# The first layer's function as a clamped square: one ScalarE pass and two VectorE passes from PSUM, in a new order

## The chip, the cores and the metric

The kernel runs on one core of one Trainium2 chip. The metric is the device time of one execution in microseconds (us), as the median of several runs. Engines are TensorE (PE; PEld are its weight loads), VectorE (DVE), ScalarE (ACT), GpSimd (POOL) and SyncE (SP), which issues the DMAs here.

## What is computed

An attention with a memory term over 4 batches of 8 heads, 576 positions and 64 channels, followed by two feed-forward layers of 512 to 2048 to 512 channels over the 2304 rows. The first one has the function that this change is about:

```
h = x @ w_in
g = where(h >= 1, h, where(h <= -1, 0, (h + 1)**2 / 4))
x = g @ w_out
```

The second layer is `(max(h, 0) + alpha * min(h, 0)) @ w_out`. All is float32 outside; inside, the matrices are held as a high and a low float16 half, and each product is made of three float16 products (high by high, high by low, low by high).

## The kernel before

The work is written once in Python as named sections: `p` prepares a batch, `a` attends, `w` converts weights, `s` makes the scales, `u` is the first layer's first product with its function, `d` its second product, `t` and `f` the second layer. A planner (`Plan`) collects the instructions and puts them in order before anything is issued: `schedule` is a list scheduler that walks over time with a cost for each instruction, and `RANK` is a written list of 534 section parts that gives the priorities, and so the order in which each engine gets its instructions. Where an instruction may run on several engines (`plan.either`), the table `HOME` fixes the engine for some of them, and the planner picks for the rest. Instructions inside `with plan.ahead()` stand before all others in the ranking. On the chip each engine works through its own list in order.

A batch has two chunks of 288 columns. `up1` makes, for each of eight `fq`, a PSUM tile `h` of 128 x 2 x 288 (two banks) out of 24 products of `w1i` with `x`. PSUM tiles with the tag `f` have two buffers; `h`, the outputs `y` of `down1` and the tiles of the second layer share them. The function needs the tile `h` and scales that are given by channel: `su`, `sd` (128 x 8, one column for each `fq`), `bu` and `c` (one column). It is worked out like this, with everything scaled by a power of two so that float16 holds it:

```
A.activation(out=u, in_=ps[:, :, :n], func=AF.Relu, scale=su[:, fq : fq + 1], bias=bu[:, 0:1])
A.activation(out=d, in_=ps[:, :, :n], func=AF.Prelu, scale=sd[:, fq : fq + 1], bias=bu[:, 1:2], alpha=0.5)
shift(d, c)
V.scalar_tensor_tensor(out=u, in0=u, scalar=c, in1=d, op0=ALU.min, op1=ALU.mult)
split(u, gh, gl)
```

Two ScalarE passes read PSUM, `shift` adds `c` to `d` on ScalarE, VectorE or GpSimd, and VectorE multiplies. `split` copies `u` to float16 (`gh`, on any of the three) and subtracts it (`gl`, on GpSimd or VectorE). `u` and `d` are in SBUF, 128 x 576 float32, with two buffers each. `down1` then multiplies `g` with `w1o`, 4 x 48 products a chunk. `scales1` works out the small scale tiles once a batch. `attend` makes scores `s`, their exponentials `e`, probabilities `p` (transposed by DMA into `pt`, or on TensorE into `tt` for the first batch) and the attention products `px`. The four first-layer batches and the weights for the second layer are interleaved with the attention of the later batches; the second layer comes last.

Every line of the profile is line 424 (where the planned instructions are issued), so tiles tell the instructions apart.

Of the kernel before, what the change touches and what calls it, by code (L numbers as in the profile page):

```python
# [1222 lines left out]
a1C2.2 u01.1 a1C2.4 a1C2.1 a1C3.1 d00.o3 w1i3.3 a1C3.0 s3 a1C1.1 a1C1.0 a1C3.2 a1C1.2 a2C0.1 p1.3 d10 w1o0.3 a1C3.4
a0B1 a1C3.3 w1o1.s0 w1o2.1 d00.o2 u01.4 u01.0 p2.s u01.6 d01.o1 w1i1.s0 u01.5 w1i1.s1 d01.o0 a2C1.2 a2C1.1 u10.4
a2C1.0 w1o1.2 a2C0.2 a2C1.3 a2C1.4 a2C0.4 a2C0.3 d01.o3 a2C3.3 a2C3.0 d01.o2 a2C0.0 u10.6 a2C3.4 u10.1 u10.0 a2C2.1
a2C3.2 u10.2 a2C3.1 u10.3 a2C2.0 w1o1.0 p2.0 u10.5 u11.1 u10.7 d10.o0 a2C2.4 d10.o1 a2C2.2 a2C2.3 w1o3.2 a3C0.0 a3C1.3
u11.6 m3.0 d10.o2 u11.3 a3C0.1 p3.s w1o0.0 a3C1.4 w1i3.s1 d10.o3 d21 u11.5 w1o3.s0 u11.7 a3C0.2 w2i0.0 m3.2 u11.0
a3C0.x4 a3C1.0 u11.2 u11.4 d11.o0 d11.o1 m1.2 w2i0.a a0B2.x4 a3C0.4 a3C0.3 w1i1.0 d11.o3 u20.3 a3C3.4 a3C1.1 u20.4
w1i0.2 m3.1 a3C1.2 a1C2.q w1i3.s0 p2 a3C2.2 a1C2 a3C1 w1i2.3 u21.2 a3C2.1 w2i0.1 a3C3.q d11.o2 a2C0.q u20.7 a0B2
a3C2.x2 m1.1 u20.0 w2i0.s1 a2C0.x2 a3C2.4 m2.1 a3C3.3 u21.3 w2i2.s1 a0A2.x2 a3C2.0 u20.5 w1i2.s0 d11 u20.1 a3C3.1  # L1230
w2i0.m a3C1.x2 u20.2 u21.7 a3C2.x4 a2C0.x4 u20.6 a3C0.q a3C3.0 a2C2.q w2i2.0 a2C1.q u21.4 d20.o0 d20.o3 p2.3 w1i0.3
w1o3.s1 d20.o1 u21.5 d20.o2 a3C3.2 a1C1 a1C0.x2 u21.1 w2i2.a a3C2.3 w2i1.s0 w2i3.3 u21.0 u21.6 w2i2.m d21.o0 w2i1.s1
w2i1.a d21.o1 u30.1 d21.o2 a1C1.x4 d21.o3 u30.0 u30.6 u31.2 w2i2.2 m3.3 w2i3.a w1o1.1 w2i2.s0 w2i1.2 w2i3.s0 w1i3.a
f01 u30.4 w2i3.m c u30.2 u30.7 a2C3.x2 u30.3 m2.2 u31.1 w1o1.3 w2o3.a w1o2.3 w2i2.1 p2.1 w2i1.m u30.5 w2o0.1 u31.5
d30.o2 d30.o0 w2o3.m f00 w1o0.s0 w2o0.a d30.o1 d30.o3 w2o3.3 a1C3 w2o3.2 u31.0 a2C0 w2i1.3 w2o0.m w2i3.2 w2o1.m u31.7
w1o2.2 p2.2 a3C1.q u31.3 u31.4 f00.2 f00.3 u31.6 f00.7 a2C1 d31.o1 f00.6 w2o2.2 s1 d31.o0 w2o0.s0 d31.o3 w2o3.s0
d31.o2 w2o3.s1 w1i2.a f00.1 a2C3 w1o1.s1 a2C2 w1o3.3 f00.4 f00.0 a0A0 f01.7 f00.5 f01.5 f01.6 p3.1 d01 d30 f00.o1
# [152 lines left out]
```

## Time and profile before

| | |
|---|---|
| median of 3 runs | 1044.4 us (1041.12 to 1047.64) |
| profiled execution | 1042.5 us, span of its instructions 1040.6 us |
| TensorE busy | 947.1 us, 91% of the span |
| VectorE, ScalarE, GpSimd busy | 684.7, 515.6, 375.7 us |
| mean granted TensorE clock | 0.993 of full speed |

The busy time of an engine is the time in which one of its instructions ran. TensorE does nearly the same products whatever the function; the time in which it is idle is what the rest of the kernel adds. Times in windows are counted from the start of the span.

### The profile page before, as it was taken

To read this page: it belongs to the slowest core of one execution; us is meant where nothing else is said; L and a number is where in the kernel's file an instruction comes from. 1 tells how busy PE (TensorE), PEld (TensorE's weight loads), DVE (VectorE), ACT (ScalarE), POOL (GpSimd) and SP (SyncE) were. 2 spreads that over 40 slices of the span, in tenths; PEclk is the share of its full clock that TensorE was granted. 3 is DMA by queue.
4 is the path that set the end of the run, shared out by engine and by line. 5 is a ranking of instruction groups with operands and counts; after the bars stand their busy time and mean duration, and the time that the engine had idled before them with its cause. 6 is when DMAs were issued, how large, how long until landed. Compare 5 with 4: busy or idle time off the path is not lost.

```text
span 1040.6 us, 20570 instructions
## 1 busy us (share of the span) xinstructions
PE 947.1 (91%) x8043; PEld 709.2 (68%) x8043; DVE 684.7 (66%) x1803; ACT 515.6 (50%) x1030; POOL 375.7 (36%) x405
## 2 busy tenths in 40 slices
PE   2178779999999999999989999999999999999998
PEld 1156446666667666766667777777777777777776
DVE  6979989989887788987877889892323413042320
ACT  5458777667566663765456646332322423131220
POOL 1353554667466673543533521251010111100020
PEclk9999988999999999999999999999999999999999
DMA  9833324567755774376654152320001000000000
GB/s 334 291 113 122 135 89 135 129 133 184 164 126 112 162 164 94 71 157 124 118 145 146 48 171 82 129 86 24 30 18 35 12 13 12 24 1 23 7 18 23
DMA packets 132096, 104.23 MB, mean 100 GB/s; under 512 B 98464, under 2 KB 113312, under 8 KB 132000
## 3 DMA queue, kind: packets, MB, share of 16 engines
q1 hardware_dynamic: 132000, 102.93, 36.9%
q8 instruction: 63, 1.03, 0.4%
q14 instruction: 33, 0.27, 0.1%
HBM read 66.73 MB, written 9.44 MB: 73 GB/s over the span
## 4 chain that ended last, share of the span: by engine, by line
PE 40%; DVE 4%; DMA 3%; POOL 2%; issue 2%; ACT 1%; SPq 0%; ACTq 0%; POOLq 0%
PE h L424 21%; PE o L424 17%; PE y L424 3%; DMA pt<-p 1%; DMA w2o_raw<-in_w2o 1%; DVE u L424 1%; DMA w2i_raw<-in_w2i 1%; POOL d L424 1%; POOL w2o L424 0%; DVE p L424 0%; ACT u L424 0%; DVE yt L424 0%; DMA yr<-y 0%; POOL p L424 0%; ACT d L424 0%
## 5 line engine op out<-in xcount | busy, mean ns | idle before, releaser
L424 PE MATMUL y<-g,w1o 128*128 128x288 f16 x1536 | 203.7, 286 | 1.8 <-DVE g L424 1.5
L424 PE MATMUL h<-x,w1i 128*128 128x288 f16 x1536 | 200.5, 286 | 4.6 <-ACT d L424 2.1
L424 PE MATMUL h<-yt,w2i 128*128 128x288 f16 x1536 | 194.8, 286 | 1.3 <-ACT u L424 1.3
L424 PE MATMUL o<-g,w2o 128*128 128x288 f16 x1536 | 193.9, 286 | 0.5 <-POOL w2o L424 0.5
L424 DVE SCALAR_TENSOR_TENSOR u<-u,al 128x288 f32<-128x288 f32 x128 | 67.0, 555 | 186.8 <-ACT u L424 186.6
L424 PEld LDWEIGHTS <-w1i 128*128 128x128 f16 x1536 | 146.9, 98 | 50.9 <-issue 12.7
L424 PEld LDWEIGHTS <-w1o 128*128 128x128 f16 x1536 | 145.0, 98 | 51.3 <-issue 12.6
L424 PEld LDWEIGHTS <-w2i 128*128 128x128 f16 x1536 | 150.1, 98 | 39.3 <-issue 1.5
L424 PEld LDWEIGHTS <-w2o 128*128 128x128 f16 x1536 | 150.1, 98 | 38.6 <-POOL w2o L424 0.8
L424 POOL TENSOR_TENSOR g<-u,g 128x576 f16<-128x576 f32 x54 | 74.1, 1372 | 182.7 <-ACT g L424 132.6
L424 ACT ACTIVATE e<-e,mxt 128x576 f32<-128x576 f32 (+4 forms) x160 | 88.3, 553 | 65.6 <-DVE mxt L424 55.1
L424 ACT ACTIVATE u<-h,sa 128x288 f32<-128x288 f32 x128 | 58.5, 498 | 125.5 <-PE h L424 122.3
L424 POOL TENSOR_SCALAR g<-u 128x576 f16<-128x576 f32 x40 | 30.5, 764 | 213.4 <-DVE u L424 156.9
L424 PE MATMUL s<-qk 64*128 64x288 f32 (+4 forms) x384 | 89.7, 481 | 15.8 <-DVE mxt L424 14.2
L424 DVE TENSOR_TENSOR g<-u,g 128x576 f16<-128x576 f32 x74 | 59.9, 810 | 31.5 <-ACT g L424 18.7
L424 ACT ACTIVATE oe<-o,osc 128x288 f32<-128x288 f32 x32 | 16.0, 501 | 111.4 <-PE o L424 111.4
L424 DVE SCALAR_TENSOR_TENSOR u<-u,c,d 128x576 f32<-128x576 f32 x64 | 59.7, 934 | 14.4 <-POOL d L424 10.1
L424 DVE CUSTOM_DVE_ANT_0 e<-s,mask 128x288 f32<-128x288 f32 (+4 forms) x160 | 64.3, 419 | 6.6 <-PE s L424 4.2
L424 PEld LDWEIGHTS s<-qk 64*128 64x128 f32 x384 | 40.0, 203 | 42.0 <-DVE mxt L424 27.4
L424 ACT ACTIVATE u<-h,bu,su 128x576 f32<-128x576 f32 x64 | 52.8, 825 | 21.8 <-PE h L424 16.6
L424 ACT ACTIVATE g<-u 128x576 f16<-128x576 f32 x61 | 41.6, 681 | 43.8 <-DVE u L424 23.2
L424 DVE SCALAR_TENSOR_TENSOR p<-e,sm,p 128x320 f16<-128x320 f32 (+4 forms) x80 | 57.0, 730 | 8.2 <-POOL p L424 5.8
(221 smaller groups left out, 1247.4 us busy)
## 6 DMA issues: line engine op xcount, KB each, us to landing
ring<-in_w1i SPq DMA_DIRECT2D x16, 512.0 KB, 6.2
w1o_raw<-in_w1o SPq DMA_DIRECT2D x16, 512.0 KB, 3.7
w2i_raw<-in_w2i SPq DMA_DIRECT2D x16, 512.0 KB, 3.8
w2o_raw<-in_w2o SPq DMA_DIRECT2D x16, 512.0 KB, 3.8
qk<-in_qk SPq DMA_DIRECT2D x12, 576.0 KB, 4.6
qn<-in_qn SPq DMA_DIRECT2D x16, 320.0 KB, 3.4
vc<-in_vc SPq DMA_DIRECT2D x16, 320.0 KB, 4.3
y<-ye SPq DMA_DIRECT2D x32, 144.0 KB, 2.5
```

What stands on the lines that cost most here:

```text
L424: fn(*args, **kw)
```

## The change

The function is worked out as the larger of two values: the product times a scale, and the square of the product after it was clamped to the two limits (where h is -1 and 1). VectorE clamps the tile out of PSUM into `d`, with two limits by channel (`lim`, new in `scales1`); ScalarE squares `d` in place, with scale and bias by channel; VectorE reads PSUM a second time, scales it and takes the larger of it and `d`. `shift` goes. `bu` has one column instead of two, `sd` has the scale `c` twice, and `sc[b]` holds `lim` where `c` was. `RANK` and `HOME` are replaced as a whole. Among the parts `uNN.N` and `dNN.oN` and `fNN` of `RANK`, a first-layer tile follows another directly in 46 places before and in 43 after. Of the instructions of `u` parts that `HOME` fixes, copies to float16 were 18 on ScalarE, 11 on VectorE and 22 on GpSimd and are 17, 14 and 17; subtractions were 29 on VectorE and 16 on GpSimd and are 22 and 23.

```diff
@@ -512,15 +512,6 @@
                 V.tensor_copy(out, src)
             else:
                 V.tensor_scalar(out=out, in0=src, scalar1=scale, scalar2=None, op0=ALU.mult)
-
-        plan.either(*(lambda e=e: way(e) for e in engines))
-
-    def shift(t, by, engines=(A, V, G)):
-        def way(e):
-            if e is A:
-                A.activation(out=t, in_=t, func=AF.Identity, bias=by)
-            else:
-                e.tensor_scalar(out=t, in0=t, scalar1=by, scalar2=None, op0=ALU.add)
 
         plan.either(*(lambda e=e: way(e) for e in engines))
 
@@ -993,22 +984,32 @@
         V.tensor_scalar(
             out=ig.bitcast(I32), in0=f, scalar1=float(-2 * ONE23), scalar2=float(381 * ONE23), op0=ALU.mult, op1=ALU.add
         )
-        bu = tiny.tile([P, 2], F32, tag="bu", name=f"bu_{b}")
-        V.tensor_scalar(out=bu[:, 0:1], in0=c, scalar1=0.5, scalar2=None, op0=ALU.mult)
-        V.tensor_scalar(out=bu[:, 1:2], in0=c, scalar1=-1.0, scalar2=None, op0=ALU.mult)
+        bu = tiny.tile([P, 1], F32, tag="bu", name=f"bu_{b}")
+        V.tensor_scalar(out=bu, in0=c, scalar1=0.5, scalar2=None, op0=ALU.mult)
+
+        lim = tiny.tile([P, 2, 8], F32, tag="lim", name=f"lim_{b}")
+        V.tensor_scalar(
+            out=lim[:, 1].bitcast(I32),
+            in0=inv1.bitcast(I32),
+            scalar1=-1.0,
+            scalar2=float(254 * ONE23),
+            op0=ALU.mult,
+            op1=ALU.add,
+        )
+        V.tensor_scalar(out=lim[:, 0], in0=lim[:, 1], scalar1=-1.0, scalar2=None, op0=ALU.mult)
         su = tiny.tile([P, 8], F32, tag="su", name=f"su_{b}")
         sd = tiny.tile([P, 8], F32, tag="sd", name=f"sd_{b}")
-        V.tensor_scalar(out=su, in0=inv1, scalar1=bu[:, 0:1], scalar2=None, op0=ALU.mult)
-        V.tensor_scalar(out=sd, in0=inv1, scalar1=c, scalar2=None, op0=ALU.mult)
+        V.tensor_scalar(out=su, in0=inv1, scalar1=bu, scalar2=None, op0=ALU.mult)
+        V.tensor_scalar(out=sd, in0=inv1, scalar1=c, scalar2=c, op0=ALU.mult, op1=ALU.mult)
         ym = tiny.tile([P, NCH * EB], F32, tag="ym", name=f"ym_{b}")
-        sc[b] = (c, ig, bu, su, sd, ym)
+        sc[b] = (lim, ig, bu, su, sd, ym)
 
     def split(u, gh, gl):
         copy(gh, u, None, (A, V, G))
         combine(gl, u, gh, ALU.subtract)
 
     def up1(b, ch, w_in, tags=("g", "g", "g", "g")):
-        c, ig, bu, su, sd, ym = sc[b]
+        lim, ig, bu, su, sd, ym = sc[b]
         x = x_t[b][ch]
         n = CHS[ch][1]
         g = []
@@ -1023,19 +1024,25 @@
             u = buf([P, 2, n], F32, "u", f"u{b}_{ch}_{fq}")
             d = buf([P, 2, n], F32, "d", f"d{b}_{ch}_{fq}")
             with plan.ahead():
-                A.activation(out=u, in_=ps[:, :, :n], func=AF.Relu, scale=su[:, fq : fq + 1], bias=bu[:, 0:1])
-
-
-                A.activation(
-                    out=d, in_=ps[:, :, :n], func=AF.Prelu, scale=sd[:, fq : fq + 1], bias=bu[:, 1:2], alpha=0.5
+
+
+                V.tensor_scalar(
+                    out=d,
+                    in0=ps[:, :, :n],
+                    scalar1=lim[:, 0, fq : fq + 1],
+                    scalar2=lim[:, 1, fq : fq + 1],
+                    op0=ALU.max,
+                    op1=ALU.min,
                 )
-                shift(d, c)
-                V.scalar_tensor_tensor(out=u, in0=u, scalar=c, in1=d, op0=ALU.min, op1=ALU.mult)
+                A.activation(out=d, in_=d, func=AF.Square, scale=su[:, fq : fq + 1], bias=bu)
+                V.scalar_tensor_tensor(
+                    out=u, in0=ps[:, :, :n], scalar=sd[:, fq : fq + 1], in1=d, op0=ALU.mult, op1=ALU.max
+                )
                 split(u, gh, gl)
         return g
 
     def down1(b, ch, g, w_out, w_out_inv):
-        c, ig, bu, su, sd, ym = sc[b]
+        lim, ig, bu, su, sd, ym = sc[b]
         ysc = tiny.tile([P, 4], F32, tag="ysc", name=f"ysc_{b}_{ch}")
         V.tensor_scalar(out=ysc, in0=w_out_inv, scalar1=ig, scalar2=None, op0=ALU.mult)
         n = CHS[ch][1]
@@ -1215,119 +1222,112 @@
 ORDER = _order()
 
 RANK = """
-w1i0.m w1i1.3 u00.0 m1.0 w1i0.s0 s0 a0A1.q d00 p0.1 w1i0.s1 a0A0.x2 w1i0.1 a0A1.0 a0A1.1 a0A0.1 p0.3 a0A0.q a0A3.q
-w1i0.a a0A0.0 p0.s w1i1.m a0A1.2 a0A0.2 a0A2.1 a0A2.0 w1i0.0 l w1i2.m a0A2.2 m1.3 p0 a0A3.0 w1o0.a w1i1.1 a0A3.1
...
+m1.3 w1i0.m p0.3 a0A0.0 l a0A0.x2 s0 a0A1.2 a0A0.1 p0.s d00 a0A1.0 w1i1.m a0A1.1 w1i0.s0 a0A0.2 a0A2.1 a0A3.0 w1i1.3
+a0A2.2 w1i0.s1 a0A3.1 w1i2.m a0A2.0 u00.0 w1i1.1 w1i0.a a0A3.2 a0A0.q p0.0 p1 p0.1 a0B0.3 u00.6 u00.1 a0B0 d10 m1.0
...
```

## Rows read from the trace of the kernel before

**Rows 1.** windows: length; busy us of PE, PEld, DVE, ACT, POOL; clock; DMA share, GB/s
```profile
0.00:94.60 94.60, 44.09 (x225) 28.77 (x225) 74.36 (x254) 54.78 (x125) 33.07 (x45) 1.00 0.67 232
94.60:182.00 87.40, 70.52 (x514) 48.24 (x514) 81.02 (x217) 67.27 (x114) 41.70 (x33) 0.92 0.33 112
182.00:640.00 458.00, 437.29 (x4090) 317.57 (x4089) 382.23 (x1061) 281.46 (x581) 241.59 (x277) 1.00 0.56 130
640.00:1040.60 400.60, 395.25 (x3219) 314.57 (x3216) 147.08 (x272) 112.08 (x212) 59.35 (x52) 1.00 0.10 32
```

**Rows 2.** TensorE's waits, 94.6 to 182 us: total, times, longest
```profile
PE s L424 <- DVE mxt L424: 5.7, 4, 1.8
PE px L424 <- ACT tt L424: 2.5, 2, 1.8
PE w1o_pm L424 <- DVE w1o_mg L424: 2.3, 1, 2.3
```

**Rows 3.** TensorE's waits, 182 to 640 us
```profile
PE px L424 <- DMA pt<-p: 6.9, 9, 1.4
PE s L424 <- DVE mxt L424: 3.9, 6, 1.1
PE px L424 <- DVE x L424: 2.6, 3, 1.4
```

**Rows 4.** TensorE's waits, 0 to 94.6 us
```profile
PE pt L424 <- POOL pf L424: 15.7, 1, 15.7
```

**Rows 5.** groups of instructions by form: count, busy us, mean ns, idle before
```profile
L424 ACT ACTIVATE u<-h,bu,su 128x576 f32<-128x576 f32 x64 | 52.8, 825 | 21.8 <-PE h L424 16.6 <-DVE g L424 1.9 <-DVE w2o_mg L424 1.4
L424 ACT ACTIVATE d<-h,bu,sd 128x576 f32<-128x576 f32 x64 | 52.7, 824 | 4.6 <-PE h L424 4.5
L424 ACT ACTIVATE d<-d,c 128x576 f32<-128x576 f32 x33 | 25.5, 772 | 0.4
L424 POOL TENSOR_SCALAR d<-d,c 128x576 f32<-128x576 f32 x16 | 29.4, 1835 | 13.4 <-ACT d L424 11.9 <-issue 1.4
L424 DVE TENSOR_SCALAR d<-d,c 128x576 f32<-128x576 f32 x15 | 9.3, 620 | 1.9 <-ACT d L424 1.6
L424 DVE SCALAR_TENSOR_TENSOR u<-u,c,d 128x576 f32<-128x576 f32 x64 | 59.7, 934 | 14.4 <-POOL d L424 10.1 <-ACT d L424 2.8 <-ACT u L424 0.8
```

**Rows 6.** groups by form on VectorE, passes that read PSUM
```profile
L424 DVE TENSOR_SCALAR x<-px,xs 128x288 f16<-128x288 f32 x5 | 2.5, 505 | 0.0
L424 DVE SCALAR_TENSOR_TENSOR x<-px,xs,x 128x288 f16<-128x288 f32 x16 | 8.1, 509 | 3.3 <-ACT x L424 3.2
L424 DVE CUSTOM_DVE_ANT_0 e<-s,mask 128x448 f32<-128x448 f32 x32 | 19.3, 613 | 1.0 <-PE s L424 0.9
L424 DVE CUSTOM_DVE_ANT_0 e<-s,mask 128x288 f32<-128x288 f32 x32 | 13.9, 445 | 1.6 <-POOL p L424 1.1 <-PE s L424 0.4
```

**Rows 7.** groups by form on ScalarE
```profile
L424 ACT ACTIVATE oe<-o,osc 128x288 f32<-128x288 f32 x32 | 16.0, 501 | 111.4 <-PE o L424 111.4
L424 ACT ACTIVATE w1i<-w1i_t,w1i_s 128x1024 f16<-128x1024 f32 x4 | 4.6, 1138 | 0.4 <-DVE w1i_t L424 0.4
```

**Rows 8.** instructions of tile d: duration ns min/median/max
```profile
L424 DVE SCALAR_TENSOR_TENSOR u<-u,c,d x64: 797/818/1839, 100.6 to 641.3; 128x576 f32<-128x576 f32 x64
```

**Rows 9.** windows, instructions of tile d: length; busy us of DVE, ACT, POOL
```profile
94.60:182.00 87.40, 7.91 (x9) 9.65 (x12) 6.40 (x3) 0.92 0.33 112
182.00:640.00 458.00, 60.15 (x69) 67.32 (x84) 22.97 (x13) 1.00 0.56 130
```

**Rows 10.** ScalarE's timeline near 583 us: start, us
```profile
583.04 0.83 ACT L424 ACTIVATE d<-h,bu,sd 128x576 f32<-128x576 f32 x1 [0.58 <-PE h L424]
583.78 0.82 ACT L424 ACTIVATE u<-h,bu,su 128x576 f32<-128x576 f32 x1
```

**Rows 11.** chain that ended last, near 583 us: start, us
```profile
583.12 2.94 PE h L424 x24
```

**Rows 12.** groups by form on ScalarE, table loads
```profile
L424 ACT ACT_TABLE_LOAD x1 | 1.3, 1283 | 0.7 <-PEq L1379 0.7
```

More of the change, by code (lines that the diff above doesn't have):

```diff
@@ L1223 @@
[L1223 to L1237, printed above, removed]
@@ L1328 @@
[L1328 to L1330 removed]
+w1i0.0:1=dve w1i0.1:1=act w1i0.s0:1=pool w1i0.s0:2=pool w1i0.3:1=act a0A0.0:1=act a0A0.0:3=dve a0A0.1:2=act
+a0A0.1:3=pool a0A0.1:4=act a0A0.2:1=dve a0A0.2:2=act a0A0.2:3=dve a0A0.2:4=dve a0A0.x2:1=dve a0A0.x2:3=act
@@ new lines @@
+w1i1.1:1=act w1i1.s0:2=dve w1i1.2:1=act w1i1.s1:1=pool a0A1.0:2=act a0A1.1:1=dve a0A1.1:3=pool a0A1.1:4=act
+a0A1.2:1=pool a0A1.2:3=pool a0A1.2:4=act a0A1.x2:1=dve w1i2.0:1=dve w1i2.s0:2=dve w1i2.2:1=dve w1i2.3:1=dve
+w1i2.s1:1=dve w1i2.s1:2=dve a0A2.0:1=act a0A2.0:4=dve a0A2.1:2=pool a0A2.2:2=pool a0A2.2:4=act a0A2.x2:3=dve
+w1i3.1:1=act w1i3.s0:1=pool w1i3.s0:2=dve w1i3.2:1=dve w1i3.3:1=act w1i3.s1:1=act a0A3.0:2=act a0A3.0:3=dve
+a0A3.0:4=act a0A3.1:1=dve a0A3.1:3=dve a0A3.1:4=act a0A3.2:3=dve a0A3.x2:1=act a0A3.x2:3=act u00.0:2=pool u00.1:1=pool
@@ new lines @@
+u00.2:1=act u00.3:1=pool u00.4:1=pool u00.5:1=dve u00.6:1=act u00.7:1=act u00.7:2=pool w1o0.0:1=dve w1o0.s0:1=act
+w1o0.2:1=act w1o0.3:1=act w1o0.s1:1=act w1o0.s1:2=dve w1o1.0:1=act w1o1.s0:2=dve w1o1.2:1=act w1o1.3:1=dve
+w1o1.s1:1=pool w1o1.s1:2=dve w1o2.1:1=act w1o2.2:1=act w1o2.3:1=act w1o3.0:1=dve w1o3.1:1=dve w1o3.s0:2=dve
+w1o3.2:1=act w1o3.s1:2=dve a0B0.3:3=pool a0B0.4:1=act a0B0.4:3=pool a0B0.4:5=dve a0B0.x4:1=act a0B1.3:2=dve
+a0B1.3:3=pool a0B1.4:1=dve a0B1.4:2=act a0B1.4:3=dve a0B1.4:5=act a0B2.3:1=pool a0B2.3:3=dve a0B2.3:4=act a0B2.4:2=act
@@ new lines @@
+a0B2.4:3=pool a0B2.4:4=dve a0B3.3:2=pool a0B3.3:3=pool a0B3.4:2=dve a0B3.4:3=pool a0B3.4:4=act a0B3.4:5=act
+a0B3.x4:1=act u01.0:1=act u01.0:2=dve u01.1:1=act u01.1:2=pool u01.2:1=act u01.2:2=dve u01.3:1=act u01.4:1=act
+u01.4:2=pool u01.5:2=dve u01.6:1=dve u01.7:1=pool a1C0:1=pool a1C0.0:1=pool a1C0.0:3=act a1C0.0:4=dve a1C0.0:5=pool
+a1C0.0:6=dve a1C0.1:1=act a1C0.1:3=act a1C0.1:6=pool a1C0.2:1=dve a1C0.2:3=act a1C0.2:5=pool a1C0.2:6=dve
+a1C0.x2:3=act a1C0.3:2=pool a1C0.3:3=dve a1C0.3:4=dve a1C0.4:1=dve a1C0.4:2=pool a1C0.4:3=act a1C0.4:4=dve
@@ new lines @@
+a1C0.4:6=dve a1C0.x4:1=act a1C1:1=dve a1C1.0:1=act a1C1.0:4=dve a1C1.0:5=pool a1C1.0:6=dve a1C1.1:1=dve a1C1.1:2=pool
+a1C1.1:4=pool a1C1.2:1=pool a1C1.2:3=pool a1C1.2:5=act a1C1.2:6=pool a1C1.x2:1=dve a1C1.3:1=dve a1C1.3:2=pool
+a1C1.3:3=pool a1C1.3:4=dve a1C1.3:5=pool a1C1.4:1=act a1C1.4:2=dve a1C1.4:4=dve a1C1.4:5=pool a1C1.x4:1=dve
+a1C2.0:3=dve a1C2.0:4=pool a1C2.0:5=pool a1C2.1:1=dve a1C2.1:2=pool a1C2.1:5=pool a1C2.2:1=act a1C2.2:2=dve
+a1C2.2:3=pool a1C2.2:5=pool a1C2.2:6=pool a1C2.x2:1=act a1C2.3:1=act a1C2.3:2=dve a1C2.3:3=pool a1C2.3:5=act
@@ new lines @@
+a2C2.1:6=dve a2C2.2:2=dve a2C2.2:3=pool a2C2.2:4=dve a2C2.2:5=dve a2C2.2:6=pool a2C2.x2:1=act a2C2.x2:3=dve
+a2C2.3:1=dve a2C2.3:2=dve a2C2.3:4=dve a2C2.3:5=act a2C2.4:2=dve a2C2.4:3=pool a2C2.4:6=pool a2C2.x4:1=act a2C3:1=dve
+a2C3.0:1=pool a2C3.0:2=pool a2C3.0:3=act a2C3.0:4=pool a2C3.0:6=dve a2C3.1:1=dve a2C3.1:4=pool a2C3.1:6=pool
+a2C3.2:1=dve a2C3.2:2=pool a2C3.2:3=act a2C3.2:5=pool a2C3.x2:1=act a2C3.x2:3=dve a2C3.3:1=pool a2C3.3:4=dve
+a2C3.3:5=dve a2C3.3:6=pool a2C3.4:1=pool a2C3.4:2=pool a2C3.4:3=act a2C3.4:4=dve a2C3.4:6=dve a2C3.x4:1=act
@@ new lines @@
+u10.0:1=dve u10.0:2=dve u10.1:1=pool u10.2:1=act u10.3:1=dve u10.3:2=dve u10.4:1=act u10.4:2=pool u10.5:1=pool
+u10.5:2=pool u10.6:2=dve u10.7:2=dve u11.0:2=dve u11.1:2=dve u11.2:1=dve u11.2:2=pool u11.3:1=dve u11.3:2=pool
+u11.4:2=dve u11.5:2=pool u11.6:2=pool u11.7:1=pool a3C0.0:1=pool a3C0.0:2=dve a3C0.0:4=dve a3C0.0:5=act a3C0.0:6=pool
+a3C0.1:1=dve a3C0.1:2=dve a3C0.1:5=pool a3C0.1:6=pool a3C0.2:1=act a3C0.2:3=pool a3C0.2:6=pool a3C0.3:1=act
+a3C0.3:2=dve a3C0.3:3=pool a3C0.3:5=pool a3C0.3:6=pool a3C0.4:1=dve a3C0.4:3=pool a3C0.4:4=dve a3C0.4:5=dve
@@ new lines @@
+a3C0.x4:1=act a3C1:1=dve a3C1:2=dve a3C1.0:1=pool a3C1.0:2=pool a3C1.0:3=dve a3C1.0:4=dve a3C1.0:5=pool a3C1.1:1=dve
+a3C1.1:2=dve a3C1.1:3=pool a3C1.1:4=dve a3C1.1:5=dve a3C1.1:6=pool a3C1.2:3=act a3C1.x2:1=act a3C1.x2:3=act
+a3C1.3:2=pool a3C1.3:3=act a3C1.3:4=dve a3C1.3:6=pool a3C1.4:1=act a3C1.4:2=dve a3C1.4:3=act a3C1.4:4=dve a3C1.4:5=dve
+a3C1.4:6=dve a3C2:1=act a3C2:2=dve a3C2.0:1=pool a3C2.0:3=act a3C2.0:4=pool a3C2.0:5=pool a3C2.1:3=act a3C2.1:4=dve
+a3C2.1:6=pool a3C2.2:1=dve a3C2.2:3=dve a3C2.2:4=pool a3C2.2:6=dve a3C2.x2:3=act a3C2.3:1=dve a3C2.3:3=dve
@@ new lines @@
+a3C2.3:4=pool a3C2.3:5=pool a3C2.3:6=pool a3C2.4:1=dve a3C2.4:2=pool a3C2.4:4=dve a3C2.4:5=pool a3C2.4:6=dve
+a3C2.x4:1=act a3C3:1=pool a3C3:2=dve a3C3.0:2=dve a3C3.0:3=pool a3C3.0:5=dve a3C3.0:6=pool a3C3.1:2=pool a3C3.1:3=dve
+a3C3.1:4=pool a3C3.1:5=act a3C3.2:1=pool a3C3.2:2=dve a3C3.2:4=dve a3C3.2:5=act a3C3.x2:1=act a3C3.x2:3=act
+a3C3.3:1=dve a3C3.3:4=dve a3C3.3:5=act a3C3.4:2=dve a3C3.4:4=pool a3C3.4:5=pool a3C3.4:6=pool a3C3.x4:1=act
+u20.0:1=dve u20.0:2=pool u20.1:1=dve u20.1:2=pool u20.2:1=pool u20.2:2=pool u20.3:1=act u20.4:1=act u20.4:2=pool
@@ new lines @@
+u20.5:1=pool u20.5:2=dve u20.6:1=pool u20.6:2=dve u20.7:1=act u20.7:2=dve u21.0:2=dve u21.1:1=dve u21.2:1=dve
+u21.3:1=pool u21.3:2=pool u21.4:1=dve u21.4:2=dve u21.5:1=dve u21.5:2=pool u21.6:1=act u21.6:2=dve u21.7:2=dve
+w2i0.0:1=act w2i0.1:1=dve w2i0.s0:1=act w2i0.2:1=act w2i0.3:1=dve w2i0.s1:2=dve w2i1.0:1=act w2i1.s0:1=act
+w2i1.s1:1=act w2i2.0:1=act w2i2.1:1=dve w2i2.s0:1=act w2i2.2:1=dve w2i2.3:1=act w2i3.1:1=dve w2i3.s0:1=pool
+w2i3.2:1=dve w2i3.3:1=dve w2i3.s1:1=act w2i3.s1:2=pool u30.0:1=pool u30.0:2=dve u30.2:1=pool u30.2:2=dve u30.3:1=pool
@@ new lines @@
+f01.2:1=act f01.2:2=pool f01.4:1=pool f01.5:1=pool f01.6:2=dve f01.7:1=pool f01.7:2=dve f10.0:1=pool f10.0:2=dve
+f10.1:1=act f10.2:2=pool f10.3:2=pool f10.5:1=pool f10.5:2=dve f10.6:2=pool f10.7:1=act f11.0:1=pool f11.1:1=act
+f11.1:2=pool f11.2:2=pool f11.4:1=dve f11.4:2=dve f11.5:1=dve f11.5:2=dve f11.6:1=dve f11.6:2=dve f11.7:1=pool
+f11.7:2=dve f20.0:1=dve f20.0:2=dve f20.1:1=dve f20.1:2=pool f20.2:1=dve f20.2:2=dve f20.3:1=pool f20.3:2=pool
+f20.4:1=dve f20.4:2=pool f20.5:2=dve f20.6:1=dve f20.7:1=pool f21.0:1=act f21.0:2=dve f21.1:1=act f21.1:2=pool
@@ L1331 @@
+f21.2:1=dve f21.2:2=dve f21.3:1=act f21.3:2=pool f21.4:1=pool f21.4:2=pool f21.5:2=dve f21.6:1=dve f21.6:2=pool
+f21.7:1=pool f21.7:2=dve f30.0:1=dve f30.0:2=dve f30.1:2=pool f30.2:1=act f30.2:2=dve f30.4:1=act f30.4:2=pool
+f30.5:1=pool f30.6:1=dve f30.6:2=dve f31.0:1=dve f31.1:1=pool f31.1:2=dve f31.2:1=dve f31.2:2=dve f31.4:1=pool
+f31.4:2=dve f31.5:1=dve f31.5:2=dve f31.6:1=act f31.7:1=act f31.7:2=dve
 """.split()
```

134 lines of the change are left out of this document (43 added, 91 removed).

## The prediction

> **What bounds the kernel now.** I read the page first (TensorE busy 947.1 of 1040.6 us), then cut the span into four stretches with the windows view [rows 1], because the share of busy time hides where the gaps lie. The first stretch ends where the first-layer product starts; the second ends where the last part of that chunk's eight tiles is handled and the second chunk begins; the third ends with the last first-layer tile; the fourth is second layer alone. TensorE's idle time is 94.60 - 44.09 = 50.5 us, then 87.40 - 70.52 = 16.9, then 458.00 - 437.29 = 20.7, then 400.60 - 395.25 = 5.4: 93.5 us in all. The products themselves are not touched by the change, so the end of the kernel can move only through these gaps and through the granted clock, whose mean is 0.92 of full speed (a mixture of the 1.2 and 2.4 GHz levels) in the second stretch and 1.00 elsewhere. In that stretch VectorE is busy 81.02 of 87.40 us, 93%: it is the engine that TensorE waits on. The waits of TensorE there say the same: scores wait for row maxima from VectorE, the transposed blocks for ScalarE copies, a weight scale for VectorE, 10.5 us in these three [rows 2]. In the third stretch VectorE is busy 382.23 of 458, 83%, and TensorE's gaps are many and small: 6.9 us of 20.7 end on a DMA transpose, and at most 13.8 on a helper engine, of which 3.9 and 2.6 are the two largest [rows 3]. The fourth stretch has next to nothing to give. Of the 50.5 us of the first, 15.7 are one wait for a probability tile while the inputs stream in [rows 4]; the function that changes doesn't run there.
>
> **The four old passes.** Each of 64 tiles of 128x576 took two ScalarE reads of PSUM (52.8 and 52.7 us in all), a shift (25.5 us on ScalarE for 33 of them, 29.4 on GpSimd for 16, 9.3 on VectorE for 15) and one VectorE product of two SBUF operands (59.7 us) [rows 5]. So 131.0 us leave ScalarE, 29.4 GpSimd, and 69.0 VectorE.
>
> **The three new passes.** The trace has no VectorE pass from PSUM at 576 columns. The nearest by kind are a tensor_scalar from PSUM with a pointer scalar at 288 columns, 505 ns, and a scalar_tensor_tensor with one PSUM and one SBUF operand, 509 ns; the slope comes from the two custom passes, (613 - 445) / 160 = 1.05 ns a column [rows 6]. That gives 505 + 288 x 1.05 = 807 ns and 811 ns. From below the clamp is bounded by the row without a pointer, 613 + 128 x 1.05 = 747 ns; from above by a second pointer that costs as much again as the first (505 - 445 = 60 ns), 867 ns. I take 0.81 us for both passes, the rows that are nearest in kind: 64 x 1.62 = 103.7 us, so VectorE gains 34.7 us (between 30.8 and 38.5). For the Square, the ScalarE shift of the same size with one pointer takes 772 ns [rows 5]; a second pointer is priced by the two-pointer read at 576 columns, 825 ns, against the one-pointer read at 288, 501 ns, carried to 576 with the slope (1138 - 772) / 448 = 0.817 [rows 5, 7]: 501 + 235 = 736, so 89 ns. Square is then 0.86 us (0.77 from below), 64 x 0.86 = 55.0 us, and ScalarE is relieved of 76.0. Together the three helpers lose 76.0 + 29.4 - 34.7 = 70.7 us, and VectorE alone gets busier. The limits cost one or two more tiny VectorE instructions a batch, some 0.2 us each time, in front of the first product: I count 0.3 us in the prelude, within the error of its term.
>
> **A rule that speaks against the change.** The old product, 128x576 with both operands in SBUF, has a median of 818 ns but a mean of 934 and a maximum of 1839 [rows 5, 8]: it is often held while GpSimd works. The Trainium skill (GPSIMD Engine Reference, Specifications) says that the SBUF interfaces are shared, with contention for VectorE instructions that run in a 2-port mode or have two SBUF inputs; by it neither new pass would be held. My price already has no such wait in it, so if the rule failed here and each pass were held like the old one, VectorE would carry another 2 x 64 x 0.116 = 14.8 us. The Trainium skill (VectorE: DVE Perf Modes, Rules for kernel authors) advises, for elementwise work on a matmul's output, to accept the slow rate from PSUM or to copy it out first if several operations follow; the change reads it twice, which is the first rival below.
>
> **Where it lands.** By the windows of tile d, the second stretch holds 9 + 12 + 3 = 24 old passes, eight tiles, and the third 166, so 56 tiles nearly [rows 9]. In the second stretch VectorE changes by 8 x 1.62 - 7.91 = +5.1 us, ScalarE by -9.65 - 8 x 0.825 + 8 x 0.86 = -9.4, GpSimd by -6.4: -10.7 together. If no work is handed over, VectorE would be busy 86.1 of 87.4 us and the stretch would become longer, by up to those 5.1 us. But the copies to f16 and the remainders around these tiles have several homes, and the new table of homes chooses them anew; spread over three engines -10.7 us is -3.6 each. I take -3.6, a fifth of the 16.9 us gap; bounds are +5.1 and, with the whole gap and the 0.08 x 87.4 = 7.0 us that the granted clock cost, -24. In the third stretch VectorE changes by 56 x 1.62 - 60.15 = +30.6 us, to 412.8 of 458 (90%), ScalarE by -67.32 - 46.2 + 48.2 = -65.3, GpSimd by -23.0. There -57.7 over three engines is -19.2 each, more than the gap that helpers leave; I take -6, somewhat under half of the 13.8 us, since the DMA's 6.9 us stay and VectorE's queue gets no shorter. Bounds: -13.8, and +10 if VectorE's 90% leaves a third of its new load uncovered. For the prelude I take -2: VectorE is busy 74.36 of 94.60 us there, and since the change in the order moves every part of the attention and the weights (their DMAs on SyncE's queue too), the order can win or lose a few us; bounds -8 and +5. The second layer: 0, covered by 395 us of products in 400. The sum is -3.6 - 6 - 2 = -11.6 us. The profiled execution took 1042.5 us, 1.9 more than its span and 1.9 less than the median of the three; on its own time the sum gives 1031.
>
> **Rival one, slower: PSUM is held too long.** The tiles h have two PSUM buffers. Now ScalarE starts on a tile at 583.04, within 0.1 us of TensorE's start on the other buffer, and has read it twice at 584.60 [rows 10], while TensorE needs 2.94 us for the 24 products of the other buffer [rows 11]: 1.56 against 2.94 us. With the new passes the tile is let go only after 0.81 + 0.86 + 0.81 us and three hand-offs, each taken as 0.1 us like this one: 2.8 us. That is still below 2.94, but only if VectorE takes both passes at once, and VectorE is 90% busy, with passes of 0.4 to 0.6 us [rows 6] and longer ones in front. The point from which it decides is a mean wait over 0.15 us for a tile that follows another directly; the listed priorities have 43 such successions of first-layer tiles (46 before). At 0.4 us lost in each that is 17 us, and with the 5.1 us of the second stretch and no gain elsewhere 1042.5 + 22 = 1065; with half of the gains kept about 1059. Against it: the passes of this layer stand ahead of all others in the planner's ranking, and output products, scores and attention products lie between many of the tiles. I give it 0.11, at 1060. A smaller variant is that Square doesn't share its table with Exp: the trace has a single table load of 1.283 us [rows 12]; two of them at each of, say, 20 alternations of the two functions would be 51 us of ScalarE time, of which 20 might show: 0.03, 1062.
>
> **Rival two, no change.** ScalarE and GpSimd are relieved, but neither ends most of TensorE's waits: VectorE does, and it gets 34.7 us more. Then what the order wins, VectorE takes back, and the gaps stay at 93 us, give or take 8: 1040, between 1033 and 1050. For it: VectorE's 93% in the second stretch. Against it: GpSimd's slow shift (1835 ns a piece) leaves the chain, and the chain from product to f16 becomes shorter by a pass. I give it 0.42.
>
> **How the numbers follow.** Forecast 0.44 (1031, itself 1015 to 1033), no change 0.42, slower 0.14. The three runs of before spread over 0.6%, so 1% (10.4 us) is about what a measurement can tell from no change; the forecast lies just beyond it. The range takes in the forecast's bounds short of their far end (all gaps of both middle stretches and the clock together would give about 1000, to which I leave 0.05) and reaches past the no-change case into the start of the slow one: 1013 to 1054.
>
> **What would show it.** Right: ScalarE's busy time falls by about 76 us and VectorE's rises by 30 to 40, new passes of about 0.8 us; the gap in the second stretch shrinks below 15 us and the granted clock there rises; TensorE's waits for u or d stay below 5 us. Wrong: TensorE's wait "h on VectorE's u" becomes a large row (rival one), or VectorE is full in stretches two and three and the sum of TensorE's idle time is still over 90 us (rival two), or more than one table load on ScalarE. If the gain comes out of the first 95 us, the step that failed is mine, of where the order can win.

## The result, and the profile after

The changed kernel takes 1051.74 us (median of 18 runs, 1048.42 to 1055.84) against 1044.15 before (18 runs): ratio 1.0078, 95% interval 1.0063 to 1.0093. I had forecast 1031, faster; it is slower by 7.6 us. The profiled execution took 1054.8 us with a span of 1053.0, so in the profiled pair the difference is 12.4 us of span, more than the medians differ by.

The windows of the kernel after, cut at the same events as [rows 1] (first h of the first chunk, first h of the second chunk, end of the last first-layer tile); columns as there:

```profile
0.00:96.10 96.10, 40.15 (x226) 26.36 (x226) 78.38 (x265) 55.40 (x127) 25.61 (x36) 0.89 0.68 229
96.10:186.60 90.50, 72.74 (x513) 51.57 (x512) 82.02 (x222) 64.43 (x107) 38.86 (x29) 0.85 0.34 111
186.60:651.00 464.40, 434.23 (x4067) 314.90 (x4067) 390.23 (x1085) 226.78 (x499) 212.58 (x261) 1.00 0.56 125
651.00:1053.00 402.00, 398.35 (x3242) 316.82 (x3239) 154.11 (x291) 115.14 (x216) 49.36 (x41) 1.00 0.10 35
```

TensorE's gaps are 56.0, 17.8, 30.2 and 3.6 us, 107.5 in all; before they were 50.5, 16.9, 20.7 and 5.4. The stretches are longer by 1.5, 3.1, 6.4 and 1.4 us. The granted clock is lower in the first two, 0.89 and 0.85 where it had been 1.00 and 0.92. So half of the loss lies in the long third stretch, where the gap grew by 9.5 us, and none of the three terms that I had forecast as gains came. TensorE's busy time is 945.5 us, 1.6 less than before.

TensorE's waits over the whole span of the kernel after (total, times, longest):

```profile
PE am_pm L424 <- DVE m L424: 24.8, 2, 24.2
PE w1i_pm L424 <- DVE w1i_mg L424: 12.3, 1, 12.3
PE px L424 <- DMA pt<-p: 11.2, 10, 2.6
PE s L424 <- DVE mxt L424: 10.7, 9, 2.6
PE h L424 <- DVE u L424: 9.7, 9, 1.7
...
PE y L424 <- DVE u L424: 2.9, 4, 1.0
```

Two rows of the same view of before:

```profile
PE s L424 <- DVE mxt L424: 14.2, 15, 1.8
...
PE h L424 <- ACT d L424: 2.1, 3, 1.0
```

The two largest rows of after lie in the first stretch, where the function doesn't run; the 15.7 us for a probability tile [rows 4] are gone. Two rows are new: h and y wait for VectorE's u, 9.7 + 2.9 = 12.6 us in 13 places, 8.5 us of them in the third stretch and 4.1 in the second. Before, TensorE waited 2.1 us in 3 places for the ScalarE pass that reads the tile. What holds TensorE there is no data but the PSUM buffer, since the old holder of the buffer is the tile whose last reader is the pass that writes u. The waits for a DMA transpose have grown, 11.2 against 6.9 us [rows 3], while those for scores went down, from 14.2 to 10.7.

The first line and the three new passes on the page of the kernel after:

```profile
PE 945.5 (90%) x8043; PEld 709.6 (67%) x8043; DVE 704.7 (67%) x1862; ACT 461.8 (44%) x946; POOL 326.4 (31%) x365
...
L424 ACT ACTIVATE d<-d,bu,su 128x576 f32<-128x576 f32 x64 | 55.2, 863 | 73.3 <-DVE d L424 65.7
...
L424 DVE TENSOR_SCALAR d<-h,lim 128x576 f32<-128x576 f32 x64 | 55.8, 871 | 13.0 <-PE h L424 12.9
L424 DVE SCALAR_TENSOR_TENSOR u<-h,sd,d 128x576 f32<-128x576 f32 x64 | 52.0, 813 | 12.3 <-ACT d L424 11.0
```

ScalarE has 53.8 us less than before, GpSimd 49.3 less, VectorE 20.0 more. The clamp takes 871 ns, the Square 863 and the second pass 813.

### The profile page after: what moved, and what is told of

It reads as the page before. It is cut to its first block, busy times and chain, and to the rows that moved or that the text cites. A ratio compares the mean times of both kernels' runs of the same rounds, so it can differ in the third digit from the quotient of the medians.

```text
span 1053.0 us, 20541 instructions
## 1 busy us (share of the span) xinstructions
PE 945.5 (90%) x8043; PEld 709.6 (67%) x8043; DVE 704.7 (67%) x1862; ACT 461.8 (44%) x946; POOL 326.4 (31%) x365
## 4 chain that ended last, share of the span: by engine, by line
PE 48%; DVE 21%; DMA 16%; POOL 5%; ACT 4%; issue 4%; SPq 1%; ACTq 0%; POOLq 0%; DVEq 0%
PE h L424 23%; PE o L424 16%; DMA pt<-p 8%; PE y L424 4%; DVE e L424 3%; DVE p L424 2%; DVE u L424 2%; DVE d L424 2%; POOL p L424 2%; DMA w1o_raw<-in_w1o 2%; DMA vc<-in_vc 2%; PE px L424 1%; DMA w2i_raw<-in_w2i 1%; PE s L424 1%; DVE sm L424 1%
## 5 line engine op out<-in xcount | busy, mean ns | idle before, releaser
L424 POOL TENSOR_TENSOR g<-u,g 128x576 f16<-128x576 f32 x61 | 83.8, 1374 | 210.1 <-ACT g L424 136.6
L424 ACT ACTIVATE e<-e,mxt 128x192 f32<-128x192 f32 (+4 forms) x160 | 88.1, 552 | 60.8 <-DVE mxt L424 46.1
L424 PE MATMUL s<-qk 64*128 64x288 f32 (+4 forms) x384 | 87.2, 478 | 16.5 <-DVE mxt L424 10.7
L424 ACT ACTIVATE d<-d,bu,su 128x576 f32<-128x576 f32 x64 | 55.2, 863 | 73.3 <-DVE d L424 65.7
L424 DVE TENSOR_TENSOR g<-u,g 128x576 f16<-128x576 f32 x67 | 55.8, 834 | 35.8 <-POOL g L424 22.9
L424 POOL TENSOR_SCALAR g<-u 128x576 f16<-128x576 f32 x32 | 22.0, 686 | 177.2 <-DVE u L424 113.3
L424 DVE CUSTOM_DVE_ANT_0 e<-s,mask 128x192 f32<-128x192 f32 (+4 forms) x160 | 64.0, 419 | 5.4 <-PE s L424 3.9
L424 DVE SCALAR_TENSOR_TENSOR p<-e,sm,p 128x320 f16<-128x320 f32 (+4 forms) x87 | 60.5, 715 | 6.5 <-POOL p L424 3.4
L424 DVE TENSOR_SCALAR d<-h,lim 128x576 f32<-128x576 f32 x64 | 55.8, 871 | 13.0 <-PE h L424 12.9
L424 DVE SCALAR_TENSOR_TENSOR u<-h,sd,d 128x576 f32<-128x576 f32 x64 | 52.0, 813 | 12.3 <-ACT d L424 11.0
```

The lines of the kernel that those rows point to most:

```text
L424: fn(*args, **kw)
```

## The experiments

Three theories. Hold: a tile h stays in PSUM through three passes on two engines (that time is called the hold), and TensorE waits for the buffer. Load: VectorE, already full where TensorE waits on it, has 20 us more to do. Order: the new `RANK` and `HOME` are themselves the worse.

In the first four runs the planner planned each kernel anew. In the later ones the order of instructions is kept as it was in the kernel they start from: the plan is made with the old instruction, and an operand or a call is replaced afterwards; in their traces TensorE's 8043 instructions stand in the same order as in that kernel. The kernel before was measured again beside each group: 1043.29 us with the first four runs, 1044.64 with the next four and 1044.03 with the last four. The changed kernel was not. The edits below are shortened.

**Function and order taken apart.** The new function with the old `RANK` and `HOME`, and the old function with the new ones:

```diff
 # first run: up1 and scales1 of the new kernel
-RANK, HOME of the kernel after
+RANK, HOME of the kernel before, u parts: key 2 -> 1, key 3 -> 2
 # second run: up1 and scales1 of the kernel before
-RANK, HOME of the kernel before
+RANK, HOME of the kernel after, u parts: key 1 -> 2, key 2 -> 3
```

> The new function with the order of the kernel before (RANK and HOME of before, the keys of the u parts renumbered because the shift is gone). Theory hold (the tile h stays in PSUM through three passes on two engines, and TensorE waits for the buffer): TensorE waits at least 10 us for VectorE's u whatever the order, so 1050 to 1060. Theory order (the replaced RANK and HOME lose the time, in the prelude and at the DMA transposes): 1040 to 1046, with the waits on u small. Theory load (VectorE has 20 us more to do): 1048 to 1056, with the loss spread over waits for scores and x and few waits on u. An order that only fits its own function would show as slower than the changed kernel here.

> The old function with the new RANK and HOME (the keys of the u parts renumbered, the shift left to the planner). Theory hold: no waits of TensorE on u, and the time near before, 1042 to 1048. Theory order: it keeps the loss, 1050 to 1055. Theory load: as before, 1042 to 1048. An order that only fits its own function: 1050 or more, with new waits that are in neither of the two kernels.

Measured: 1077.65 us, ratio 1.0319 (1.0287 to 1.035), and 1081.76 us, ratio 1.0375 (1.0351 to 1.04). Both mixtures are some 26 us or more above either of the two kernels, outside what any of the three theories gave them. What came is the fourth case of the expectations, an order that only fits its own function: neither the function nor the order explains the result by itself. TensorE's waits, first run, then second:

```profile
PE s L424 <- DVE mxt L424: 20.8, 19, 3.2
...
PE h L424 <- DVE u L424: 6.9, 8, 2.7
```

```profile
PE s L424 <- DVE mxt L424: 27.0, 14, 6.0
```

The wait on u comes with the function (6.9 us with the old order), and the largest wait in both is for the scores' maxima from VectorE, 20.8 and 27.0 us. Not all of the loss is waiting: TensorE's busy time is 962.3 and 964.5 us against 947.1 before, at a mean granted clock of 0.968 and 0.959 against 0.993. These two runs say little of the change itself, because a new plan costs tens of microseconds by itself. The next two bear that out.

**A tiny instruction, with and without a hold.** In the kernel before, behind the last pass:

```diff
                 V.scalar_tensor_tensor(out=u, in0=u, scalar=c, in1=d, op0=ALU.min, op1=ALU.mult)
+                last = tiny.tile([P, 1], F32, tag="last", name=f"last{b}_{ch}_{fq}")
+                V.scalar_tensor_tensor(
+                    out=last, in0=ps[:, 0, 0:1], scalar=1.0, in1=u[:, 0, 0:1], op0=ALU.mult, op1=ALU.mult
+                )  # control: in0=d[:, 0, 0:1]
```

> The kernel before with one tiny VectorE instruction more for each of the 64 tiles, on one column, which reads the finished u and the PSUM tile, so that the tile is held until after the last pass. VectorE gets about 64 x 0.2 = 13 us more. Theory hold: 8 to 15 us slower than the same kernel whose tiny instruction reads d instead of PSUM, and TensorE's wait on that instruction is a row of about 10 us. Theories load and order: the same as that kernel within 3 us.

> The control: the same tiny instruction reads u and d, both in SBUF, so PSUM is let go as before. Theory hold: 1044 to 1048. Theory load: 64 small instructions, some 13 us of VectorE, cost 4 to 8 us, 1048 to 1052.

Measured: 1093.46 us (ratio 1.0481, 1.0454 to 1.0508) with the hold, 1068.83 (1.0251, 1.0229 to 1.0273) for the control. The two differ by 24.6 us, more than I expected of the hold. But each was planned anew, and their TensorE instructions differ in order from the 326th on, so the difference is for hold and plan together. The control alone lost 25.5 us, far over the 4 to 8 that theory load gave it. The run with the hold shows the wait by name:

```profile
PE h L424 <- DVE last L424: 26.0, 16, 4.2
...
PE y L424 <- DVE last L424: 7.2, 5, 2.6
```

**The same tiny instruction in the old order.** To see how much of the control's loss was the new plan:

```diff
+                plan.ops[-1].ways["dve"][0].append(  # issued behind the product, unknown to the planner
+                    (nc.vector.scalar_tensor_tensor, (), dict(out=last, in0=d[:, 0, 0:1], in1=u[:, 0, 0:1], ...)))
```

> The kernel before with its order kept, and the tiny instruction of the control run (u and d, one column) put behind each of the 64 products without the planner knowing of it. If the control's 25 us came from planning anew, this stays at 1043 to 1048. If they came from VectorE's 64 instructions (theory load), it is 1060 or more.

Measured: 1052.49 us, ratio 1.0062 (1.0035 to 1.0089). That lies between the two expectations. So some 16 to 18 us of the control's 25.5 came from planning anew, and 8 from the instruction, which takes longer than I had thought:

```profile
L424 DVE SCALAR_TENSOR_TENSOR last<-d,u 128x1 f32<-128x1 f32 x64 | 18.1, 284 | 2.2
```

The 18.1 us of added instructions cost 8 us, 0.43 us for each, so even without a new plan VectorE's time is not free. But VectorE's busy time rose by only 8.2 us (692.9 against 684.7), and the loss is mostly no wait: in the profiled execution, the slowest of the eight and 13.5 us longer than that of before, TensorE's idle time grew by 3.2 us and its products took 10.2 us longer (957.3 against 947.1), at a mean granted clock of 0.984 against 0.993.

**More load, no hold.** Again in the kernel before, order kept, half a pass more behind each product:

```diff
+                plan.ops[-1].ways["dve"][0].append(
+                    (nc.vector.scalar_tensor_tensor, (), dict(out=d[:, 0], in0=d[:, 0], in1=u[:, 0], ...)))
```

> The kernel before with its order kept and one more VectorE pass of half the size (128x288, both operands in SBUF, about 0.52 us) behind each of the 64 products: 33 us more for VectorE, as much as I had predicted for the change, and no longer hold of PSUM. Theory load: 12 us slower or more, 1055 to 1075. Theory hold: at most 6 us, 1044 to 1050, no row of TensorE on u.

Measured: 1067.56 us, ratio 1.0212 (1.0175 to 1.025). The added pass, then TensorE's largest wait:

```profile
L424 DVE SCALAR_TENSOR_TENSOR d<-d,u 128x288 f32<-128x288 f32 x64 | 37.5, 586 | 2.2
```

```profile
PE s L424 <- DVE mxt L424: 23.4, 23, 4.5
```

37.5 us of VectorE cost 23 us, 0.61 for each. In the profiled pair TensorE's idle time grew by 17.9 us and its products took 5.6 longer. The largest part of the idle time is waits for the scores' maxima, 23.4 us against 14.2: a full VectorE delays what stands behind the added passes. As expected by theory load, and against hold alone.

**More hold, no load.** In the kernel before, order kept, the last pass reads PSUM:

```diff
-                in0=u, scalar=c, op0=ALU.min, op1=ALU.mult
+                in0=ps[:, :, :n], scalar=su[:, fq : fq + 1], op0=ALU.mult, op1=ALU.min
```

> The kernel before with its order kept; the last VectorE pass reads the PSUM tile where it read u (product by scale and smaller of it and d, so the function is left out), with the same size and one PSUM operand instead of SBUF. VectorE's load is the same; the tile is held from the product to the end of the fourth pass, about 1.6 us more or longer. Theory hold: 10 to 25 us slower than before, 1053 to 1068, nearly all of it in a new wait of TensorE on u. Theories load and order: 1041 to 1046.

Measured: 1065.14 us, ratio 1.0182 (1.0147 to 1.0218): 20.5 us slower although VectorE is busy 15.4 us less (669.3 against 684.7 us). Its waits, and the replaced pass:

```profile
PE h L424 <- DVE u L424: 22.9, 18, 3.3
...
PE y L424 <- DVE u L424: 6.0, 10, 1.9
```

```profile
L424 DVE SCALAR_TENSOR_TENSOR u<-h,su,d 128x576 f32<-128x576 f32 x64 | 51.9, 812 | 20.6 <-POOL d L424 11.6 <-ACT d L424 5.6 <-ACT u L424 1.5
```

22.9 + 6.0 us of waits on u are there that were not, so the hold by itself is enough to slow the kernel, as theory hold says and load and order do not. It is a longer hold than the changed kernel's, over four passes, the shift among them: from the end of a tile's last product to the end of the last pass that reads it the median is 4.15 us, there 3.71. So this run shows the mechanism, and not its size in the change.

**The hold taken out of the changed kernel, first try.** Order kept; the second pass reads `d` for the PSUM tile:

```diff
-                    out=u, in0=ps[:, :, :n], scalar=sd[:, fq : fq + 1], in1=d, op0=ALU.mult, op1=ALU.max
+                    out=u, in0=d, scalar=sd[:, fq : fq + 1], in1=d, op0=ALU.mult, op1=ALU.max
```

> The changed kernel with its order of instructions kept (planned as it was, one operand replaced afterwards): the second VectorE pass reads d where it read the PSUM tile, so the tile is let go after the clamp, 0.87 us, while VectorE and ScalarE do as many passes of the same size as before. The larger of product and square is left out of the result. Theory hold: TensorE's waits on u (9.7 + 2.9 us in the changed kernel) go, and the time falls by 8 to 13 us, to 1038 to 1044. Theories load and order: 1048 to 1053, the waits move to other rows.

Measured: 1057.19 us, ratio 1.0112 (1.0078 to 1.0146), so no gain at all, against theory hold. The waits on u are gone from the list, but others have grown, and the pass itself:

```profile
PE s L424 <- DVE mxt L424: 15.0, 16, 2.7
...
PE px L424 <- DVE x L424: 5.0, 5, 2.6
```

```profile
L424 DVE SCALAR_TENSOR_TENSOR u<-d,sd 128x576 f32<-128x576 f32 x64 | 62.2, 972 | 12.0 <-ACT d L424 10.7 <-POOL g L424 0.3
```

972 ns where the PSUM form took 813, 64 x 0.159 = 10.2 us more in this pass: of its 64 instances, 35 overlap a GpSimd instruction, and 18 of these take over 830 ns, while none of the other 29 takes over 820. So the edit had added a load as it took the hold away. The Trainium skill (GPSIMD Engine Reference, Specifications) names VectorE instructions with two SBUF inputs as ones in contention on the shared interfaces, and these rows agree.

The load is not all. VectorE's busy time rose by 6.2 us in sum, and in the profiled pair TensorE's idle time even fell, from 107.5 to 102.1 us; but its products took 6.8 us longer (952.3 against 945.5), 5.0 of them in the first layer's first product. The mean granted clock was 0.972 against 0.977. Why the low clock fell on more of the products here was not separated. The next try takes a pass of one SBUF operand.

**The hold taken out, second try, and the load, alone and together.** The second pass as a tensor_scalar with an accumulator; the clamp on half of the columns; both:

```diff
 # no hold
-                V.scalar_tensor_tensor(out=u, in0=ps[:, :, :n], scalar=sd[:, fq : fq + 1], in1=d, op0=ALU.mult, op1=ALU.max)
+                V.tensor_scalar(out=u, in0=d, scalar1=sd[:, fq : fq + 1], op0=ALU.mult, op1=ALU.add, accum_out=junk)
 # half clamp
-                V.tensor_scalar(out=d, in0=ps[:, :, :n], ...)
-                A.activation(out=d, in_=d, func=AF.Square, ...)
+                V.tensor_scalar(out=d[:, 0], in0=ps[:, 0, :n], ...)
+                A.activation(out=d[:, 0], in_=d[:, 0], func=AF.Square, ...)
+                A.activation(out=d[:, 1], in_=d[:, 0], func=AF.Copy)
```

> The changed kernel with its order kept; the second VectorE pass is a tensor_scalar of d with an accumulator, one SBUF operand instead of PSUM and SBUF, so that PSUM is let go after the clamp and the pass isn't stretched by GpSimd as in the first run without a hold (there 972 ns instead of 813). The larger of product and square is left out. Hold alone: 1038 to 1043. Load alone (VectorE's queue sets the pace): 1049 to 1053, the waits on u turn into waits for scores and x. Both, in parts: 1044 to 1048.

> The changed kernel with its order kept; the clamp does only the first half of the columns (0.57 instead of 0.87 us), ScalarE squares that half and copies it to the other in two short passes (about 0.25 us more than before), so that the hold stays as long and VectorE has 64 x 0.30 = 19 us less, its busy time that of the kernel before. The function of the other half is left out. Load alone: with 0.45 to 0.6 us for each us of VectorE, as the runs with added passes gave, 1040 to 1044. Hold alone: 1049 to 1053.

> Both of the edits before this: no hold and 19 us less for VectorE, order kept. If the two add up: the sum of their two gains, 1028 to 1038. If one is behind the other (the buffer is held because VectorE's queue is long): no better than the better of the two by more than 3 us.

Measured: 1040.86 us (ratio 0.9969, 0.9951 to 0.9986) without the hold, 1047.01 (1.0036, 1.0018 to 1.0054) with the half clamp, 1036.89 (0.9931, 0.9908 to 0.9954) with both. Against the changed kernel's 1051.74 that is -10.9, -4.7 and -14.9 us. The first is what hold alone gave, the second lies between load alone and hold alone, and the two add up to -15.6, nearly the third. In the profiled run without a hold, the fastest of its twelve, TensorE's idle time is 92.2 us against 107.5, and its products took 3.9 us less. The two tries without a hold differ by 16.3 us for 6.8 us of VectorE, more than any load run gives; of the 20.6 us between their profiled spans 10.7 are product time, and what set the clock apart stays open. In the run without a hold VectorE is as busy as in the changed kernel (704.1 against 704.7 us), and its second pass as long:

```profile
L424 DVE TENSOR_SCALAR_CACHE_REDUCE u<-d,sd 128x576 f32<-128x576 f32 x64 | 51.7, 807 | 11.5 <-ACT d L424 10.1 <-POOL g L424 0.3
...
L424 DVE DVE_READ_ACCUMULATOR u<-d,sd 128x1 f32 x64 | 5.2, 81 | 0.0
```

No row of TensorE on u is left in it. With the half clamp VectorE's busy time falls to 688.5 us, 16.2 us less, and the wait on u stays:

```profile
PE h L424 <- DVE u L424: 8.0, 8, 1.5
...
PE y L424 <- DVE u L424: 2.4, 4, 1.0
```

So the hold was worth 10.9 us and VectorE's load 0.2 to 0.3 us for each us; the waits on u fell a little too with the half clamp, from 12.6 to 10.4 us, so not all of its 4.7 us need be load. Both together gained 4.0 us over the better one alone, with an interval of some 3 us either way: that speaks against one being hidden behind the other, narrowly.

**A version that beats both.** The kernel before, order kept, all shifts on ScalarE:

```diff
         plan.either(*(lambda e=e: way(e) for e in engines))
+        for calls, _ in plan.ops[-1].ways.values():
+            calls[:] = [(nc.scalar.activation, (), dict(out=t, in_=t, func=AF.Identity, bias=by))]
```

> A version meant to beat both: the kernel before with its order kept and all 64 shifts on ScalarE, which was half idle: VectorE has 9.3 us less, GpSimd 29.4 less, ScalarE 24 more. Nothing is left out. Load alone: 4 to 8 us faster than before, 1036 to 1041. Hold alone: 1042 to 1046.

Measured: 1035.47 us, ratio 0.9925 (0.9898 to 0.9951), 8.6 us faster than before and 16 faster than the change, a little more than theory load gave. Its first line on the page, and its shifts among the groups by form:

```profile
PE 945.0 (92%) x8043; PEld 708.6 (69%) x8043; DVE 671.7 (65%) x1788; ACT 535.1 (52%) x1061; POOL 344.5 (33%) x389
```

```profile
L424 ACT ACTIVATE d<-d,c 128x576 f32<-128x576 f32 x64 | 49.3, 770 | 0.5
```

VectorE is busy 13.0 us less, GpSimd 31.2 less and ScalarE 19.5 more. It takes from the change what was good in it, a lighter GpSimd and no shift on VectorE, without a longer hold (median 2.13 us from the last product to the end of the last read, 2.15 before). Which of the two engines' relief paid more was not separated.

## Why the prediction was wrong

**The bound and where the gaps lie: right.** Products took the same time, 945.5 us for 947.1; the result is in TensorE's gaps, which grew from 93.5 to 107.5 us. Both signs that I had named for being wrong came: the wait of h on u, and idle time over 90 us with VectorE full. The range holds the measured time only because it reached into the slow rival's case; the forecast's own bounds (1015 to 1033) do not.

**The prices of the passes: nearly right.** The clamp measured 871 ns for 807 taken, 4 ns over my upper bound for two pointers; the second pass 813 for 811; the Square 863 for 860. The two VectorE passes cost 107.8 us, 38.8 more than the old ones, at my upper bound of 38.5. VectorE's busy time rose by only 20.0 us, because its other work took 18.8 us less in the new order. One table load remained, so the small variant with Square in another table is out.

**The failing step: the hold had no term in the sum.** I wrote that the tile is let go after 2.8 us, "still below 2.94, but only if VectorE takes both passes at once", gave that rival 0.11, and put nothing for it into the -11.6 us. Its mechanism is what happened. The passes and the hand-offs between them were nearly right: 2.7 us by my numbers, and over the 64 tiles a median of 2.76 us from the clamp's start to the end of the second pass. What failed is the wait in front of the clamp, taken as 0.1 us: over all tiles it has a median of 0.48 and a mean of 0.73 us, well over the 0.15 us from which I had said that the rival decides. The passes have a tail besides (mean 3.15 us, longest 7.05). From the end of a tile's last product, as the profile models it, to the end of the last pass that reads it the median went from 2.15 to 3.71 us; 16 of the 64 tiles were over 2.94 us before and 48 after. Each engine has its own list in order, and the passes meet other work there. The price that I had given it, 17 us, was 0.4 us in 43 places; TensorE waited 12.6 us, nearly 1 us in each of 13.

One of the long ones. Near 100 us, on VectorE, ScalarE and TensorE of the kernel after (start, us):

```profile
100.58 0.87 DVE L424 TENSOR_SCALAR d<-h,lim 128x576 f32<-128x576 f32 x1
101.37 1.82 DVE L424 SCALAR_TENSOR_TENSOR w1i_t<-w1i_t,ring 128x512 int32<-128x512 int32 x1
103.39 0.69 DVE L424 SCALAR_TENSOR_TENSOR w1o_t<-w1o_t,w1o_raw 128x512 int32<-128x512 int32 x1 [0.20 <-ACT w1o_t L424]
104.15 0.82 DVE L424 SCALAR_TENSOR_TENSOR u<-h,sd,d 128x576 f32<-128x576 f32 x1
```

```profile
102.68 0.69 ACT L424 ACTIVATE w1o_t<-w1o_raw 128x512 f32<-128x512 f32 x1 [2.19 <-POOL w1o L424]
103.25 0.86 ACT L424 ACTIVATE d<-d,bu,su 128x576 f32<-128x576 f32 x1
```

```profile
100.16 3.11 PE L424 MATMUL h<-x,w1i 128*128 128x288 f16 x24
105.02 6.05 PE L424 MATMUL h<-x,w1i 128*128 128x288 f16 x48 [1.75 <-DVE u L424]
```

The clamp starts at 100.58 and ends near 101.4. The Square starts at 103.25, as ScalarE's list had a weight conversion before it that was waiting for GpSimd. The second pass ends at 104.97, and TensorE's next product starts at 105.02, after 1.75 us of idling. That tile was held 4.4 us from the clamp's start, where two ScalarE passes of before took 1.56 [rows 10]. Taking the hold out, with the order kept and VectorE as busy, gave 10.9 us; putting a longer one into the kernel before cost 20.5.

**The gains in stretches two and three: a step that failed too.** I spread the net relief over three engines (-3.6 and, in part, -19.2 us each). VectorE's share never came: it stayed 82.02 of 90.5 us busy in the second stretch and 390.23 of 464.4 in the third. The load runs put 0.2 to 0.6 us on each us of VectorE, so its 20.0 us more are worth, by estimate, some 4 to 12 us of loss, which I had let the relief of the other two cancel. I had counted the relief of ScalarE and GpSimd as if it could be exchanged for VectorE's time.

**What the relief did give.** Without the hold the changed kernel is 3.2 us faster than before, and without hold and with VectorE near its old load (686.1 us against 684.7) 7.1 us. The relief of the other engines and the new order together were thus worth some 7 us, somewhat more than half of my 11.6: right in sign and too large. No run separates the two.

**The prelude** was forecast at -2 and is +1.5 us. It doesn't contain the function, so this is the new order; the mixtures show that order and function can't be told apart by exchanging them. The lower granted clock ahead of the function was not there with the old order: over the first 90 us it was 1.00 before and in the new function with the old order, 0.98 in the old function with the new order, and 0.92 after. Where that of the second stretch comes from stays open, as it was low in both mixtures (0.84 and 0.75 from 90 to 186 us, against 0.93 before and 0.83 after). A copy of the tile out of PSUM by ScalarE ahead of both VectorE passes, which would shorten the hold without leaving anything out, was not tried; its last pass would have two SBUF operands, like the one of 972 ns above.

## What to carry to other kernels

When a PSUM tile is read by passes on different engines, count the hold from the last product to the end of the last pass, each change of engine with the work that stands in front of it in that engine's list, and compare it with the time in which TensorE fills the other buffer. If the margin is a few tenths of a microsecond, the hold is the forecast, not a rival. Sum engines' times apart: a microsecond taken from an engine with slack doesn't pay for one put on the engine that others wait for; the shortest way to a gain here was to move 15 short passes off VectorE and 16 slow ones off GpSimd, in an order left alone. And a tuned order belongs to its kernel: test an edit in the order kept before planning anew, or the new plan's loss hides the edit. Last, compare TensorE's busy time between two runs as well as its idle time: in the first try without a hold the idle time fell by 5.4 us, and the kernel was no faster, as the products took 6.8 us longer.
